# A fused linear-attention and SwiGLU kernel: the gates of the last tiles taken in PSUM in a fixed ScalarE order, and a reordered load stage

## The chip, the cores and the metric

The kernel runs on one core of a Trainium2 chip. The metric is the device time of one execution in microseconds (us). Before the change the median of three runs is 1623.3 us (1622.49, 1623.55, 1623.3). The engines are TensorE (PE; its weight loads are PEld), VectorE (DVE), ScalarE (ACT), GpSimd (POOL) and SyncE (SP, which issues most DMAs).

## The reference

```python
def _A_ref(x, wqkv, w_phi, wo):                    # S=2048, D=576, 32 heads of 18
    q, k, v = ...(x @ wqkv)
    pq, pk = einsum(q, w_phi), einsum(k, w_phi)
    phi_q = concat([softmax(pq), softmax(-pq)]);  phi_k = the same of pk
    o = (phi_q @ (phi_k^T v)) / (phi_q @ sum(phi_k) + 1e-6)
    return o @ wo

def _B_ref(x, w_gate, w_up, w_down):               # F=4608
    return (silu(x @ w_gate) * (x @ w_up)) @ w_down

xn = layernorm(x)
out = x + _A_ref(xn, ...) * silu(_B_ref(xn, ...))
```

All inputs are fp32. x is 2048 x 576, w_gate and w_up 576 x 4608, w_down 4608 x 576.

## The kernel before, in words

**Precision.** Every fp32 operand of a matmul is kept as two rounded parts, a high part (a cast, mostly on ScalarE) and a low part (the operand less the high part, on VectorE or GpSimd). A product is then three matmuls: high x high, high x low, low x high. D = 576 is four chunks of 128 and a remainder of 64; two 32-row halves of the remainder are stacked with their low parts in one chunk, so that the remainder takes one 96-row matmul (`split_rows` L63 and the 32-row subtractions L66, L223, L278 make that chunk).

**Load stage** (L158 to L285, the first 67 us). Rows of x come in four blocks of 512 (four tiles `xn` of 128 rows each), in the order 2, 3, 0, 1. `norm_stats` (L179 to L193) takes the statistics of a tile on VectorE, then for a whole set of tiles one square root on ScalarE (L188) and five small VectorE steps. `norm_block` (L195) scales the tiles alternately on VectorE (L201) and ScalarE (L198), GpSimd repeats the last 64 columns (L204), PE transposes (L213) into PSUM tiles `tp`, three buffers, and ScalarE and VectorE split the result into `X` tiles (L215, L216). For the third transposed tile ScalarE casts two pieces (L220), copies the tile to `xr` in SBUF (L221), and GpSimd subtracts the 32 rows (L223); `xr` also goes to DRAM (L224). Between the blocks, `early_weights` (L102) splits the weights of the first two column tiles f = 0, 1 of w_gate and w_up, and `early_tile` (L119) already computes h for block pair i = 1: gate matmuls into `pe`, silu on ScalarE (L126), up matmuls into `pe`, product on VectorE (L130), store by GpSimd (L131). There, two PSUM banks `pe` alternate, so a matmul can wait for the silu or the product that empties its bank. `fold` (L235 to L243) multiplies w_k (into KVWH/KVWL) and w_q (into QH/QL) with the feature matrix PHI on PE (L242). The loop at L266 to L278 loads the six pieces of w_v into tiles `wst` (five buffers, shared with the w_q loads at L232): cast to KVWH on ScalarE (L274), KVWL on GpSimd for four (L276), the 32-row remainder on VectorE for two (L278). Behind it stand the w_q loads, the statistics of blocks 0 and 1 together, block 0, the fold of w_q, block 1. The scheduler moves what is marked high priority ahead.

**Behind it**: the k/v tiles (their first matmuls, `p`, take PSUM that the `tp` tiles held), the q tiles, and then gate/up and down products in two halves of the rows with Strassen's scheme (L741, L866). This is 67 to 1598 us.

**The end** (second half, i = 1, L862 to L913). Eight tiles of 128 rows, t = 4, 5, 6, 7, 0, 1, 2, 3, get their last two down products. `tile_of` (L882) fills a PSUM tile with the sum so far, `acc` (a ScalarE copy, L893), and adds 12 matmuls of 288 columns (`three`, L866). `finish` (L834) takes silu from PSUM to `acc` (ScalarE, L837), multiplies by the attention part (VectorE, L838), adds x (L839, VectorE for even t, GpSimd for odd ones) and stores (SP, L840). PSUM tile `pd` has two buffers. The last tile, t = 3 ("fine"), is in two halves, in `py` and `pw`, each with its own finish. Fills have high priority; the rest is in the order in which the scheduler finds it ready.

## Time and profile before

| what | value |
|---|---|
| three runs | 1622.49, 1623.55, 1623.3 us; median 1623.3 |
| the profiled execution's own time | 1622.04 us |
| its span in the trace | 1620.2 us |
| mean granted TensorE clock | 0.998 |
| PE busy | 1605.8 us, 99% of the span, 9411 instructions |
| DVE, ACT, POOL busy | 1175.9, 726.3, 660.8 us |
| DMA moved | 268.28 MB, mean 166 GB/s |

Times in the trace are microseconds from the span's start. The device time of an execution is some 1.8 us longer than its span. An engine's busy time leaves out the issue of DMAs, semaphores and branches. In a row of a timeline, the number in brackets is how long the engine had been idle and which instruction ended that; "x3" is three like instructions run together, and their time is that of the group. The lines themselves stand in the prediction.

### The profile page before, as it was taken

How to read it: one execution, taken by the hardware profiler on the slowest of the kernel's cores; microseconds unless marked ns; L12 is line 12 of the kernel's file. 1: busy time of each engine (PE TensorE's matmuls, PEld its weight loads, DVE VectorE, ACT ScalarE, POOL GpSimd, SP SyncE). 2: the span in 40 equal slices, each digit the busy share in tenths (PEclk: the TensorE clock that was granted, in tenths of full speed). 3: DMA queues.
4: the chain of work that ended last, by engine and by line, in shares of the span. 5: the costliest groups of instructions: out<-in, count | busy, mean ns of one | idle time of the engine just before them, and what ended most of it. 6: DMA issues, size and time to landing. Idle time of an engine off the chain costs nothing.

```text
span 1620.2 us, 25277 instructions
## 1 busy us (share of the span) xinstructions
PE 1605.8 (99%) x9411; PEld 1428.2 (88%) x9412; DVE 1175.9 (73%) x1727; ACT 726.3 (45%) x1399; POOL 660.8 (41%) x710
## 2 busy tenths in 40 slices
PE   9999999999999999999999999999999999999998
PEld 6899998999988888888888888888888888888887
DVE  7777769898856778877777778634667656666578
ACT  5633345544445654444444444454343333333334
POOL 3676652334115635644535435223324314133132
PEclk9999999999999999999999999999999999999999
DMA  9522243436347454555545453965445654555435
GB/s 325 172 80 82 98 144 105 125 105 191 121 158 255 165 180 163 175 171 181 177 169 191 168 188 114 335 210 148 151 137 154 187 174 157 177 181 175 142 116 176
DMA packets 121420, 268.28 MB, mean 166 GB/s; under 512 B 12754, under 2 KB 53842, under 8 KB 119506
## 3 DMA queue, kind: packets, MB, share of 16 engines
q1 hardware_dynamic: 105852, 244.73, 45.9%
q0 software_dynamic: 3552, 12.59, 2.7%
q10 hardware_dynamic: 11894, 9.35, 1.8%
q8 instruction: 74, 1.21, 0.3%
q14 instruction: 48, 0.39, 0.1%
HBM read 167.53 MB, written 99.09 MB: 165 GB/s over the span
## 4 chain that ended last, share of the span: by engine, by line
PE 94%; DVE 3%; DMA 1%; ACT 1%; issue 0%; POOL 0%; SPq 0%; POOLq 0%; ACTq 0%
PE pd L866 25%; PE px L741 25%; PE pw L741 12%; PE p L94 7%; PE py L741 6%; PE pe L94 5%; PE p L641 4%; PE kvp L320 2%; PE po L621 2%; PE vx L408 1%; PE pt L615 1%; PE vw L408 1%; PE vy L94 1%; PE vx L94 1%; DVE stats L183 1%
## 5 line engine op out<-in xcount | busy, mean ns | idle before, releaser
L866 PEld LDWEIGHTS pd<-dw,hh 128*128 128x128 f32 x3036 | 431.0, 188 | 22.3 <-DVE X L997 0.9
L866 PE MATMUL pd<-dw,hh 128*128 128x288 f32 x3036 | 446.7, 297 | 0.7 <-DVE X L997 0.4
L741 PE MATMUL px<-X,w 128*128 128x512 f32 x1512 | 390.4, 393 | 0.0
L741 PEld LDWEIGHTS px<-X,w 128*128 128x128 f32 x1512 | 275.0, 188 | 52.7 <-ACT s L770 2.2
L741 PE MATMUL pw<-X,w 128*128 128x512 f32 x744 | 191.8, 393 | 0.0
L741 PEld LDWEIGHTS pw<-X,w 128*128 128x128 f32 x744 | 139.2, 189 | 30.9
L775 DVE TENSOR_TENSOR s<-pw,s 128x512 f32<-128x512 f32 x126 | 86.5, 688 | 101.0 <-ACT s L770 89.5
L997 DVE TENSOR_TENSOR acc<-pd,acc 128x576 f32<-128x576 f32 x128 | 96.2, 752 | 84.4 <-PE pd L866 84.2
L770 ACT COPY s<-px 128x512 f32<-128x512 f32 x126 | 73.9, 586 | 160.6 <-PE px L741 160.6
L61 DVE TENSOR_TENSOR hh<-ha,hh 128x512 fp32r<-128x512 f32 x140 | 111.9, 825 | 22.8 <-ACT hh L60 21.3
L60 ACT CAST hh<-ha 128x512 fp32r<-128x512 f32 x140 | 82.7, 619 | 87.0 <-PE pd L866 72.0
L969 POOL TENSOR_TENSOR hb<-hb 128x512 f32<-128x512 f32 x34 | 46.5, 1367 | 164.9 <-DVE hb L787 159.2
L94 PE MATMUL pe<-X,wh 128*128 128x512 f32 (+1 forms) x340 | 108.5, 399 | 1.9 <-POOL X L223 0.8
L61 DVE TENSOR_TENSOR w<-ld,w 128x512 fp32r<-128x512 f32 (+1 forms) x96 | 80.2, 835 | 36.6 <-ACT w L60 35.3
L741 PE MATMUL px<-X,wt 96*128 96x512 f32 x252 | 99.5, 395 | 0.0
L741 PE MATMUL py<-X,w 128*128 128x512 f32 x378 | 98.0, 394 | 0.0
L956 POOL TENSOR_TENSOR h<-ha,hb 128x512 f32<-128x512 f32 x34 | 44.4, 1305 | 125.1 <-DVE ha L791 95.2
L982 POOL TENSOR_TENSOR ha<-ha 128x512 f32<-128x512 f32 x34 | 52.6, 1563 | 98.7 <-DVE hh L61 98.7
L60 ACT CAST w<-ld 128x512 fp32r<-128x512 f32 (+1 forms) x96 | 52.7, 549 | 88.1 <-POOL ld L729 56.4
L795 ACT COPY py<-px 128x512 f32<-128x512 f32 x63 | 36.0, 572 | 106.4 <-PE px L741 83.4
L726 POOL TENSOR_TENSOR ts<-ld 128x256 f32<-128x256 f32 x32 | 27.4, 856 | 129.4 <-issue 73.3
L741 PEld LDWEIGHTS py<-X,w 128*128 128x128 f32 x378 | 67.8, 188 | 11.3
(275 smaller groups left out, 3249.2 us busy)
## 6 DMA issues: line engine op xcount, KB each, us to landing
w_dram<-w SPq DMA_DIRECT2D x90, 512.0 KB
w<-w_dram SPq DMA_DIRECT2D x90, 512.0 KB
wt<-t_dram SPq DMA_DIRECT2D x62, 336.0 KB
ld<-in_B_w_gu SPq DMA_DIRECT2D x32, 512.0 KB
X<-sum_dram SPq DMA_DIRECT2D x8, 1280.0 KB
rt<-in_B_w_down SPq DMA_DIRECT2D x33, 288.0 KB
rb<-in_B_w_down SPq DMA_DIRECT2D x33, 288.0 KB
w_dram<-w SPq DMA_DIRECT2D x30, 256.0 KB
```

Source lines behind the costliest of these rows:

```text
L60: nc.scalar.copy(hi, src)
L61: nc.vector.tensor_sub(lo, src, hi)
L94: last = nc.tensor.matmul(ps, l, r, start=n == 0, stop=n == len(pairs) - 1)
L641: nc.tensor.matmul(ps[:, 0:HALF], a[0:w, g, jc], bw[0:w, g, n], start=k == 0, stop=k == 3 * NG - 1)
L741: nc.tensor.matmul(ps, l, r, start=first and n == 0, stop=last and n == len(mm) - 1, skip_group_check=True)
L770: snaps.append(nc.scalar.copy(t, ps))
L775: nc.vector.tensor_add(t, ps, t)
L866: nc.tensor.matmul(ps, l, r, start=first and n == 0 and m == 0, stop=n == len(hs) - 1 and m == 2, skip_group_check=True)
L956: sub(s, g["h"][0][0], g["h"][0][1])
L969: nc.gpsimd.tensor_add(a21, a21, g["h"][1][1])
L982: sub(a12, a12, g["h"][0][0])
L997: nc.vector.tensor_add(a2, pd[:, :, 0:HALF], a2)
```

## The change

Two places in the program differ; all rows between them stand in the same order on every engine.

**Load stage.** (1) For block 3 the two 32-row subtractions go from GpSimd (out of `xr`) to VectorE (out of PSUM, new L227), with high priority. (2) The w_v pieces are loaded and cast in the order (0,0), (0,1), (1,0), (1,1), (0,2), (1,2); the KVWL subtractions on GpSimd are issued behind the last remainder of the early weights. (3) The statistics and norms of block 0 are written ahead of the two remainders of KVWH, which are issued behind the sixth VectorE scaling. (4) A one-column silu is issued right behind the square root.

**End.** `finish` becomes `end`: silu in place in PSUM, product from PSUM into `acc`, adds on GpSimd, the last tile's on VectorE behind both products. A tile's end is issued behind the fill of the next but one, and a fill behind the silu of the one before. Tiles t = 6 and t = 1 use two buffers `px` in halves in place of a `pd`.

On VectorE in the load stage, where block 3's third transposed tile meets the early weights of f = 1 (`X12_66`, `X13_67` are block 3's chunks, `wl_384` and `wh_383` the split of the first weight tile, `stats`/`mv` the norms of blocks 0 and 1), before:

```order
L216 TENSOR_TENSOR X13_67<-tp_354,X13_67 128x1024
L184 BN_AGGR mv_106<-stats_105 128x2
L183 BN_STATS stats_105<-xn_414 128x6
L65 TENSOR_TENSOR wl_384<-raw_382,wh_383 128x512
L66 TENSOR_TENSOR wh_383<-raw_382,wh_383 32x2x128
L183 BN_STATS stats_105<-xn_414 128x6
```

and now:

```order
L218 TENSOR_TENSOR X13_67<-tp_354,X13_67 128x1024
L227 TENSOR_TENSOR X12_66<-tp_365,X12_66 32x512
L227 TENSOR_TENSOR X13_67<-tp_365,X13_67 32x512
L65 TENSOR_TENSOR wl_384<-raw_382,wh_383 128x512
L66 TENSOR_TENSOR wh_383<-raw_382,wh_383 32x2x128
L186 BN_AGGR mv_106<-stats_105 128x2
```

The two remainders stand directly ahead of the weight split, and one statistics step and a mean that stood ahead of it come behind.

On VectorE a little further, from the second weight tile (`wl_391`, `wh_390`) to the root, before (`h_679` is the product of an early tile, L278 makes a remainder of KVWH):

```order
L65 TENSOR_TENSOR wl_391<-raw_389,wh_390 128x512
L66 TENSOR_TENSOR wh_390<-raw_389,wh_390 32x2x128
L130 TENSOR_TENSOR h_679<-pe_664,h_679 128x512
L278 TENSOR_TENSOR KVWH_97<-wst_400,KVWH_97 32x576
L184 BN_AGGR mv_106<-stats_105 128x2
L183 BN_STATS stats_105<-xn_420 128x6
```

and now:

```order
L65 TENSOR_TENSOR wl_391<-raw_389,wh_390 128x512
L132 TENSOR_TENSOR h_680<-pe_665,h_680 128x512
L66 TENSOR_TENSOR wh_390<-raw_389,wh_390 32x2x128
L186 BN_AGGR mv_106<-stats_105 128x2
L185 BN_STATS stats_105<-xn_418 128x6
L185 BN_STATS stats_105<-xn_420 128x6
```

The product h has moved ahead of the 32-row subtraction, the remainder of KVWH is gone from here, and more of the statistics is left behind this point.

On GpSimd in the load stage, before:

```order
L204 COPY xn<-xn 128x128 x8
L131 DMA h_dram<-h 128x512
L223 TENSOR_TENSOR X_66<-xr,X_66 32x512
L223 TENSOR_TENSOR X_67<-xr,X_67 32x512
L276 TENSOR_TENSOR KVWL<-wst,KVWH 128x576 x3
L131 DMA h_dram<-h 128x512
L276 TENSOR_TENSOR KVWL<-wst,KVWH 128x576
L204 COPY xn<-xn 128x128 x6
```

and now:

```order
L206 COPY xn<-xn 128x128 x8
L133 DMA h_dram<-h 128x512
L281 TENSOR_TENSOR KVWL<-wst,KVWH 128x576 x4
L133 DMA h_dram<-h 128x512
L206 COPY xn<-xn 128x128 x2
L133 DMA h_dram<-h 128x512
L206 COPY xn<-xn 128x128 x14
```

The remainders of block 3 are gone and the four KVWL stand together. On PE, the first k/v matmul was `p_787`, which waits for a VectorE subtraction of block 1; now `p_788` comes first, and it waits for ScalarE's copy to `xr`, since its PSUM is that of the tile which this copy reads.

On ScalarE at the end (`pd`, `px`, `py`, `pw` are the PSUM tiles; a COPY is a fill, an ACTIVATE a silu), the last rows before:

```order
L837 ACTIVATE acc<-pd 128x2x288
L893 COPY pd<-acc 128x2x288
L837 ACTIVATE acc<-pd 128x2x288 x2
L837 ACTIVATE acc<-py 128x288
L837 ACTIVATE acc<-pw 128x288
```

and now:

```order
L893 ACTIVATE pd<-pd 128x2x288
L914 COPY pd<-acc 128x2x288
L893 ACTIVATE px<-px 128x288 x2
L914 COPY py<-acc 128x288
L914 COPY pw<-acc 128x288
L893 ACTIVATE pd<-pd 128x2x288
L893 ACTIVATE py<-py 128x288
L893 ACTIVATE pw<-pw 128x288
```

The fills of `py` and `pw`, which stood near the start of the end (PE ran a few of t = 3's matmuls early), now come last, and each fill is held behind the silu ahead of it.

```diff
@@ -63,7 +63,7 @@
     def split_rows(hi, lo, src):
         nc.scalar.copy(hi, src)
         nc.vector.tensor_sub(lo, src[:, :, 0:2], hi[:, :, 0:2])
-        nc.vector.tensor_sub(hi[64:96, :, 2], src[64:96, :, 2], hi[64:96, :, 2])
+        return nc.vector.tensor_sub(hi[64:96, :, 2], src[64:96, :, 2], hi[64:96, :, 2])
 
     xpool = ctx.enter_context(tc.tile_pool(name="xpool", bufs=1))
     dram = ctx.enter_context(tc.tile_pool(name="dram", bufs=1, space=bass.MemoryType.DRAM))
@@ -99,6 +99,8 @@
     pes = ctx.enter_context(ExitStack())
     eps = pes.enter_context(tc.tile_pool(name="eps", bufs=2, space=PSUM, side="right"))
 
+    rests = []
+
     def early_weights(f, *behind):
         parts = []
         for m in (0, 2):
@@ -110,7 +112,7 @@
                 for b in behind:
                     order.enter_context(tc.issue_after(b.ins))
                 with tc.high_priority():
-                    split_rows(hi, lo, raw)
+                    rests.append(split_rows(hi, lo, raw))
             parts.append((hi, lo))
         return parts
 
@@ -174,7 +176,7 @@
                         nc.sync.dma_start(xn[:, 0:D], xf[i * P:(i + 1) * P, :])
                     return xns
 
-                roots, norms = [], []
+                roots, norms, scales = [], [], []
 
                 def norm_stats(bs, xns):
                     t = slice(4 * bs[0], 4 * bs[-1] + 4)
@@ -198,8 +200,8 @@
                             norms.append(nc.scalar.activation(xn[:, 0:D], xn[:, 0:D], AF.Identity,
                                                               bias=rt[:, i:i + 1], scale=rs[:, i:i + 1]))
                         else:
-                            nc.vector.tensor_scalar(xn[:, 0:D], xn[:, 0:D], mv[:, i, 0:1], rs[:, i:i + 1],
-                                                    op0=ALU.subtract, op1=ALU.mult)
+                            scales.append(nc.vector.tensor_scalar(xn[:, 0:D], xn[:, 0:D], mv[:, i, 0:1], rs[:, i:i + 1],
+                                                                  op0=ALU.subtract, op1=ALU.mult))
                         for k in range(2):
                             nc.gpsimd.tensor_copy(xn[:, D + k * P:D + (k + 1) * P].rearrange("p (j n) -> p j n", j=4),
                                                   xn[:, 512 + 32 * k:544 + 32 * k].unsqueeze(1).to_broadcast([P, 4, 32]))
@@ -220,7 +222,11 @@
                             nc.scalar.copy(dst[m][:, 2], ps[:, m])
                         copy = nc.scalar.copy(xr, ps)
                         for m in range(2):
-                            nc.gpsimd.tensor_sub(dst[m][32:64, 2], xr[32:64, m], dst[m][32:64, 2])
+                            if b == 3:
+                                with tc.high_priority():
+                                    nc.vector.tensor_sub(dst[m][32:64, 2], ps[32:64, m], dst[m][32:64, 2])
+                            else:
+                                nc.gpsimd.tensor_sub(dst[m][32:64, 2], xr[32:64, m], dst[m][32:64, 2])
                             nc.scalar.dma_start(x_dram[i, :, :, 2 * j + m].rearrange("s p n -> p s n"),
                                                 xr[:, m].rearrange("p (s n) -> p s n", s=4))
                     return last, rest, copy
@@ -262,23 +268,26 @@
                 fold(wk, KVWH[:, :, :, 0:D], KVWL[:, :, :, 0:D])
                 _, _, copy = norm_block(3, xns[4:8])
                 first_weights.append(early_weights(1, copy))
-                wv = []
-                for n in range(6):
-                    wv.append(prep.tile([P, 6 * P], F32, name="wst", bufs=5))
-                    nc.sync.dma_start(wv[n][:, 0:D], w_v[:, n // 3, n % 3])
+                wv, places = [], [(0, 0), (0, 1), (1, 0), (1, 1), (0, 2), (1, 2)]
+                for k, c in places:
+                    wv.append(prep.tile([P, 6 * P], F32, name="wst", bufs=5)[:, 0:D])
+                    nc.sync.dma_start(wv[-1], w_v[:, k, c])
                 xns = load_x(0) + load_x(1)
-                for n in range(6):
-                    k, c = divmod(n, 3)
-                    src, vh = wv[n][:, 0:D], KVWH[:, k, c, D:2 * D]
+                for (k, c), src in zip(places, wv):
                     with tc.issue_after(copy.ins):
-                        nc.scalar.copy(vh, src)
-                    if c < 2:
-                        nc.gpsimd.tensor_sub(KVWL[:, k, c, D:2 * D], src, vh)
-                    else:
+                        nc.scalar.copy(KVWH[:, k, c, D:2 * D], src)
+                for (k, c), src in zip(places[0:4], wv):
+                    with tc.issue_after(rests[-1].ins):
+                        nc.gpsimd.tensor_sub(KVWL[:, k, c, D:2 * D], src, KVWH[:, k, c, D:2 * D])
+                norm_stats([0, 1], xns)
+                with tc.high_priority(), tc.issue_after(roots[-1].ins):
+                    nc.scalar.activation(stats[:, 0, 0, 0:1], mv[:, 0, 0:1], AF.Silu)
+                norm_block(0, xns[0:4])
+                for (k, c), src in zip(places[4:6], wv[4:6]):
+                    vh = KVWH[:, k, c, D:2 * D]
+                    with tc.issue_after(scales[5].ins):
                         nc.vector.tensor_sub(vh[64:96], src[64:96], vh[64:96])
                 wq = load_fold(1)
-                norm_stats([0, 1], xns)
-                norm_block(0, xns[0:4])
                 fold(wq, QH, QL)
                 norm_block(1, xns[4:8])
                 for f in range(2):
@@ -831,14 +840,6 @@
     def halves_of(ap):
         return ap.rearrange("p (a n) -> p a n", a=2)
 
-    def finish(t, k, pd, sx, eng):
-        r0 = HS + t * P
-        a = acc[:, t // 4 * 2:t // 4 * 2 + 2, t % 4][:, k]
-        nc.scalar.activation(a, pd, AF.Silu)
-        nc.vector.tensor_mul(a, a, halves_of(sx[:, 0])[:, k])
-        eng.tensor_add(a, a, halves_of(sx[:, 1])[:, k])
-        nc.sync.dma_start(halves_of(of[r0:r0 + P, :])[:, k], a)
-
     def late_finish(t):
 
         y = fw.tile([P, D], F32, name="ts")
@@ -879,29 +880,52 @@
                 split(w[:, 0], w[:, 1], raw[:, n])
                 ws.append(w)
 
+        silu, fills, ends = [], [], []
+
+        def end(t, pd):
+            fine = t == HT // 2 - 1
+            a = acc[:, t // 4 * 2:t // 4 * 2 + 2, t % 4]
+            s, x = (halves_of(final[t // 2][:, t % 2, m]) for m in range(2))
+            o = halves_of(of[HS + t * P:HS + t * P + P, :])
+            parts = list(enumerate(pd)) if isinstance(pd, list) else [(slice(0, 2), pd)]
+            with tc.high_priority(), tc.issue_after(fills[-1].ins):
+                for k, p in parts:
+                    silu.append(nc.scalar.activation(p, p, AF.Silu))
+                    done = nc.vector.tensor_mul(a[:, k], p, s[:, k])
+            with tc.issue_after(done.ins):
+                for k, p in parts:
+                    (nc.vector if fine else nc.gpsimd).tensor_add(a[:, k], a[:, k], x[:, k])
+                    nc.sync.dma_start(o[:, k], a[:, k])
+
         def tile_of(t, hs):
             fine = i == 1 and t == HT // 2 - 1
-            if fine:
-                pd = [fps.tile([P, BT], F32, name=n, bufs=1)[:, 0:HALF] for n in ("py", "pw")]
+            apart = fine or (i == 1 and t in (HT // 2 + 2, 1))
+            if apart:
+                names = ("py", "pw") if fine else ("px", "px")
+                both = None
+                pd = [fps.tile([P, BT], F32, name=n, bufs=names.count(n))[:, 0:HALF] for n in names]
             else:
                 both = fps.tile([P, 2, 512], F32, name="pd", bufs=2)[:, :, 0:HALF]
                 pd = [both[:, k] for k in range(2)]
             c = slice(t % 4 * P, t % 4 * P + P)
             a2 = acc[:, t // 4 * 2:t // 4 * 2 + 2, t % 4]
-            with tc.high_priority() if i else ExitStack():
-                for k in range(2 if fine else 1):
-                    nc.scalar.copy(pd[k] if fine else both, a2[:, k] if fine else a2)
+            with tc.high_priority() if i else ExitStack(), tc.issue_after(silu[-1].ins) if silu else ExitStack():
+                for k in range(2 if apart else 1):
+                    fill = nc.scalar.copy(pd[k] if apart else both, a2[:, k] if apart else a2)
+            fills.append(fill)
+            if ends:
+                ends.pop()()
             for k in range(2):
                 n = slice(k * HALF, (k + 1) * HALF)
                 three(pd[k], [(h[:, 0, c], h[:, 1, c]) for h in hs], [(w[:, 0, n], w[:, 1, n]) for w in ws],
                       False)
-                if fine:
-                    finish(t, k, pd[k], final[t // 2][:, t % 2], nc.vector)
             if i == 0:
                 nc.scalar.activation(a2, both, AF.Silu)
                 nc.scalar.dma_start(y_dram[t], a2)
-            elif not fine:
-                finish(t, slice(0, 2), both, final[t // 2][:, t % 2], (nc.vector, nc.gpsimd)[t % 2])
+                return
+            ends.append(lambda: end(t, pd if apart else both))
+            if fine:
+                ends.pop()()
 
         for r in (1, 0) if i else (0, 1):
             hs = []
```

## The prediction

> **What bounds the kernel now.** I read the page first (its span and the shares of the chain that ended last), then busy time by stretches, then the timelines of the load stage and of the end.
>
> ```profile
> span 1620.2 us, 25277 instructions
> PE 94%; DVE 3%; DMA 1%; ACT 1%; issue 0%; POOL 0%; SPq 0%; POOLq 0%; ACTq 0%
> ```
>
> TensorE is 94% of the chain. Three of the five stretches into which I cut the span (start:end, length, then the busy time of PE, PEld, DVE, ACT and POOL with counts, clock, DMA share, GB/s):
>
> ```profile
> 31.10:67.30 36.20, 33.57 (x199) 28.07 (x198) 29.41 (x52) 26.04 (x37) 18.31 (x27) 1.00 0.76 261
> 67.30:1597.80 1530.50, 1528.57 (x8948) 1366.17 (x8947) 1105.94 (x1590) 671.60 (x1320) 627.76 (x652) 1.00 0.49 160
> ...
> 1612.80:1620.20 7.40, 0.00 (x0) 0.00 (x0) 4.01 (x6) 0.41 (x2) 1.84 (x1) 0.63 0.45 159
> ```
>
> In the middle, PE is idle for 1.93 of 1530.5 us. The change leaves every engine's order there as it was, apart from the first k/v matmuls, so the middle passes on whatever shift reaches it. What can be won lies in two places: 36.20 - 33.57 = **2.63 us** of PE idle in the load stage that the change touches, and the 7.40 us behind the last matmul. All the working below is in this execution's own time (1622.04 us, span 1620.2); the difference is then taken off the median, 1623.3.
>
> **The load stage: what stands there.** PE's timeline; the bracket is the idle time before the row, and what released it.
>
> ```profile
> 35.50 0.73 PE L94 MATMUL pe<-X,wh 96*128 96x512 f32 x2 [0.83 <-POOL X L223]
> ...
> 44.11 0.47 PE L94 MATMUL pe<-X,wh 128*128 128x512 f32 x1 [0.82 <-DVE h L130]
> ...
> 48.47 0.87 PE L213 MATMUL tp<-ident,xn 128*128 128x128 f32 x3 [0.85 <-DVE xn L201]
> ...
> 54.98 5.52 PE L242 MATMUL tp<-PHI,wst 126*128 126x126 f32 x48
> ...
> 62.62 1.04 PE L213 MATMUL tp<-ident,xn 128*128 128x128 f32 x8
> ...
> 67.33 0.30 PE L94 MATMUL p<-KVWH,X 128*128 128x288 f32 x1
> ```
>
> Three stalls, 0.83 + 0.82 + 0.85 = 2.50 us, are nearly all of the idle time. VectorE and GpSimd over the same time:
>
> ```profile
> 22.42 0.42 DVE L66 TENSOR_TENSOR KVWH<-tp,KVWH 32x252 fp32r<-32x252 f32 x1
> ...
> 33.00 1.21 DVE L216 TENSOR_TENSOR X<-tp,X 128x1024 fp32r<-128x1024 f32 x1
> ...
> 34.57 1.43 DVE L65 TENSOR_TENSOR wl<-raw,wh 128x512 fp32r<-128x512 f32 x1
> 36.03 1.39 DVE L66 TENSOR_TENSOR wh<-raw,wh 32x256 fp32r<-32x256 f32 x1
> ...
> 41.72 1.53 DVE L66 TENSOR_TENSOR wh<-raw,wh 32x256 fp32r<-32x256 f32 x1
> ...
> 44.00 0.75 DVE L278 TENSOR_TENSOR KVWH<-wst,KVWH 32x576 fp32r<-32x576 f32 x1
> ...
> 44.91 0.77 DVE L183 BATCH_NORM_STATS2 stats<-xn 128x6 f32<-128x288 f32 x2
> ...
> 47.75 1.55 DVE L201 TENSOR_SCALAR xn<-xn,mv,rs 128x576 f32<-128x576 f32 x3
> ```
> ```profile
> 34.18 2.96 POOL L223 TENSOR_TENSOR X<-xr,X 32x512 fp32r<-32x512 f32 x2
> 37.31 1.43 POOL L276 TENSOR_TENSOR KVWL<-wst,KVWH 128x576 fp32r<-128x576 f32 x1 [0.17 <-POOL X L223]
> ...
> 48.46 2.47 POOL L204 COPY xn<-xn 128x128 f32<-128x128 f32 x6 [2.16 <-DVE xn L201]
> ```
>
> A 32-row subtraction of 252 elements takes 0.42 us, one of 576 takes 0.75: 1.02 ns an element, so 0.68 us for 512.
>
> **The load stage, step by step.** *Block 3's remainders.* GpSimd loses 2.96 us, VectorE gets 2 x 0.68. It starts behind the L216 that ends at 34.21: 34.9 and 35.6. PE, free at 35.50 - 0.83 = 34.67, has in the new order two more matmuls of the same tile to run first (0.73 us for two at 35.50, their latency included). I count the 0.83 us stall as gone (bounds 0.3 to 0.83).
>
> *The weight splits.* `wl` and `wh` at 34.57 and 36.03 took 1.43 and 1.39 us while GpSimd was busy. With GpSimd empty I give them the nearest uncovered prices, 0.68 and 0.42: they end at 36.7 rather than 37.42, behind two more instructions. The second tile's `wl` then waits out a KVWL to 40.0, and the product h (L130) runs at about 40.7 to 41.3, while PE comes to its bank at 44.11 - 0.82 - 0.83 = 42.5. The second stall, 0.82 us, goes, and nothing else is late there.
>
> *The KVWL subtractions* are written behind the last remainder, which is VectorE's. In the built order they carry no wait for it, only those for their load and cast. So they still run beside VectorE: about 37.2 to 40.0 for two, and two more to 43.8. Queued behind them are h's store and the xn copies (L204), and both are needed later than 43.8.
>
> *The norms.* Before, VectorE came out of wh at 43.25, then did h and one KVWH remainder, to 44.75, and the last statistics, to the root at 46.59, 1.8 us. Now h is done by 41.3, the remainder is put off, and wh ends at about 42.4. The order leaves two more statistics (0.77) and their mean behind it, so 2.65 us are still to do. The root starts at about **45.06** instead of 46.59, a gain of 1.53.
>
> ```profile
> 46.59 0.21 ACT L188 ACTIVATE rs<-mv 128x8 f32<-128x8 f32 x1 [3.94 <-DVE mv L187]
> 46.81 1.28 ACT L126 ACT_TABLE_LOAD   x1
> ...
> 52.23 1.93 ACT L215 CAST X<-tp 128x1024 fp32r<-128x1024 f32 x2
> ...
> 66.66 1.05 ACT L221 COPY xr<-tp 128x1024 f32<-128x1024 f32 x1
> ```
>
> *The silu table.* Its 1.28 us load follows the root in both programs, beside VectorE's chain. What leaves ScalarE behind it is one silu (0.3 us net of the dummy). So the cast of the first transposed pair comes at root + 5.35 rather than + 5.64, and the fold of w_q, which waits for the tile that this frees, starts 1.53 + 0.25 = 1.78 earlier, at 53.2.
>
> *What is given back.* The two KVWH remainders now stand between the scaling of xn and h on VectorE, and may exclude GpSimd's copies for 2 x 0.75, as wl and wh at 34.57 were held up beside GpSimd. I put the further PE waits there at 0.2 (bounds 0 to 0.8) and count them inside the time from 46.8 to 53.2. Block 1's transposes then come at 61.06 rather than 62.62. The first k matmul now waits for the xr copy: in this trace that copy ends at 66.66 + 1.05 = 67.71, which is 5.09 us behind the transposes' start, while p started 4.71 behind it. So the wait moves p to 61.06 + 5.12 = 66.2 instead of 67.33. PE would have been there 0.8 us sooner: this is the new stall, behind which all of k and v is queued. **Load stage: -1.1 us.** Bounds: 0, if copies and the xr copy take all, and -2.6, if all the idle time goes.
>
> **The end.** From the chain that ended last, then groups (line, engine, operation, count: shortest/median/longest in ns), then single rows of VectorE, GpSimd and SP:
>
> ```profile
> 1601.47 0.52 PE py L866 x2
> ...
> 1605.37 6.48 PE pd L866 x48
> ```
> ```profile
> L893 ACT COPY pd<-acc x7: 637/644/644, 1598.5 to 1609.3; 128x576 f32<-128x576 f32 x7
> L837 ACT ACTIVATE acc<-pd x7: 643/652/655, 1601.7 to 1611.9; 128x576 f32<-128x576 f32 x7
> ```
> ```profile
> L997 DVE TENSOR_TENSOR acc<-pd,acc x128: 740/756/759, 593.4 to 1600.1; 128x576 f32<-128x576 f32 x128
> ```
> ```profile
> 1603.21 0.75 DVE L838 TENSOR_TENSOR acc<-acc,X 128x576 f32<-128x576 f32 x1
> ...
> 1605.96 1.58 DVE L838 TENSOR_TENSOR acc<-acc,X 128x576 f32<-128x576 f32 x1 [0.54 <-ACT acc L837]
> ```
> ```profile
> 1605.50 1.43 POOL L839 TENSOR_TENSOR acc<-acc,X 128x576 f32<-128x576 f32 x1 [8.26 <-DVE acc L838]
> ...
> 1612.73 1.91 POOL L839 TENSOR_TENSOR acc<-acc,X 128x576 f32<-128x576 f32 x1 [2.21 <-issue]
> ```
> ```profile
> 1604.78 12.55 SPq L840 DMA_DIRECT2D out<-acc  x9
> ```
>
> *PE.* A tile is 12 matmuls at 6.48 / 48 = 0.135, so 1.62 us. ScalarE's fixed loop is silu 0.65 + fill 0.64 + 0.15 of latency = 1.44, and fits with 0.18 to spare. PE loses its early work on t=3, but behind the first tile it starts at 1601.5, on the split of h that releases it at 1601.47 now, with 7 x 12 = 84 matmuls to go: 1601.5 + 11.34 = 1612.84, as now (1612.8). I cost this at nothing; past the 0.18 of slack each tile would add the excess.
>
> *VectorE* multiplies from PSUM. The nearest row is L997, 756 ns over 128 instructions and never above 759, while the SBUF form took 1.58 beside a GpSimd add. So 0.75, and 7 adds leave VectorE.
>
> *GpSimd* gets the 7 adds. The first starts as the first product ends, 1603.21 + 0.75. Five whole ones at 1.43 and two in halves (4 x 0.80, from the row below) are 10.35, plus 0.3 between them: t=2's sum ends at 1614.65. This, not PE, now sets the end.
>
> ```profile
> L374 POOL TENSOR_TENSOR h<-sraw x1: 804/804/804, 83.7 to 83.7; 128x288 f32<-128x288 f32 x1
> ```
> ```profile
> L840 SPq DMA_DIRECT2D out<-acc x9: 402/534/621, 1604.8 to 1616.9; - x9
> ```
>
> *SP* issues t=2's store and the last two behind it: 0.53 + 0.40 + 0.40, to 1616.0. VectorE's last two adds (288 columns, 0.45 each by the 0.75 of a 576) are under this: pw's silu and product, some 0.45 each, are done by 1613.8, and the adds run at the latest from 1614.65 to 1615.6. Before, the last issue ended at 1604.78 + 12.55 = 1617.33; what follows, 2.87 us to the span's end, stays. **End: -1.3 us.** Bounds: -2.3 if GpSimd is never behind (products at 1613.77, one add, two issues), and +2.1 by what follows.
>
> What the adds cost depends on whether the product from PSUM holds them up. Beside products of the SBUF form an add took 1.91 at 1612.73, not 1.43; at that price seven adds take 3.4 us more, and the end is 2.1 slower instead of 1.3 faster. Against it stand the 128 rows of L997, which never met such a delay. The Trainium skill, "SBUF — State Buffer", section "SBUF: two separate sides", says that VectorE and GpSimd share one port pair as an exclusive lock, held for a whole instruction by a VectorE operation with two SBUF inputs. By that rule the product from PSUM, with one SBUF input, leaves the adds alone, and the sum keeps its 1.3; the trace agrees where it shows both, in VectorE's 1.58 at 1605.96, which ends 0.6 us behind GpSimd's 1.43 of 1605.50.
>
> **Sum.** 1.1 + 1.3 = 2.4 us: span 1617.8, profiled time 1619.6, and 1623.3 - 2.4 = **1620.9**.
>
> **The rivals.**
> - *More is won.* The xr copy is early enough because ScalarE is freer, and GpSimd hardly delays the end. For it: ScalarE has 10 us idle in the load stretch. Against it: both waits are in the built order. All 2.6 of the idle and 1.3: 1623.3 - 3.9 = 1619.4.
> - *The load stage gives nothing.* Copies blocked by the remainders and p behind xr take back what the root gains; the end's 1.3 is left: 1622.0. For it: GpSimd's copies have no slack at the third stall (xn at 47.75, its copy at 48.46, PE behind it). Against it: the root really is earlier. To this belongs the case that the change doesn't do what it says, since nothing holds the KVWL subtractions off VectorE's norms.
> - *Slower: the fourth load of w_q comes late.* Its buffer is now freed by a remainder that ends near 48.8, rather than by the last KVWL, which ends just ahead of the root, and its issue stands behind a 1280 KB store (issues, KB each, us to landing):
>
> ```profile
> a_dram<-X SPq DMA_DIRECT2D x2, 1280.0 KB
> ...
> h_dram<-h POOLq DMA_DIRECT2D x3, 256.0 KB, 4.8
> ```
>
> The fold needs it at 53.2 + 4.1 (three quarters of 5.52) = 57.3, so 8.5 us after its issue at 48.8. The nearest landing is 4.8 us for 256 KB; with 1280 KB ahead at the stretch's 261 GB/s it is up to 9.7. The gain is gone if it lands 10.9 us after its issue; at 12 us PE is 3.5 late, and the time is 1623.3 - 2.4 + 3.5 = 1624.4.
> - *Slower: the adds stretch.* GpSimd at 1.91 an add, as above, from 1.62 on already no gain at the end: 1623.3 - 1.1 + 2.1 = 1624.3. For it: the row at 1612.73. Against it: L997.
>
> **How the numbers follow.** Forecast, 1620.9: 0.42. More won, 1619.4: 0.28. Load stage nothing, 1622.0: 0.20. Late w_q, 1624.4: 0.04. Stretched adds, 1624.3: 0.04. Something else: 0.02. A measurement of this kernel can tell about 0.2%, 3.2 us, from no change. Below 1620.1 lie most of the second case and the edge of the first: faster 0.32. Above 1626.5 lies only a part of the two slower cases and of the rest: 0.04. Same: 0.64. The bounds of the terms (load 0 to -2.6, end +2.1 to -2.3) together, without the far corners that need both, give 1618.5 to 1622.8.
>
> **What would show it.** Right: no stall before the 96-row matmuls nor at h; a root near 45.1; p near 66.2 with a wait for xr ahead of it; PE's end near 1612.8 less the shift; seven GpSimd adds back to back, and the last store's issue some 3.2 us behind PE's end instead of 4.5. Wrong: the root at 46 or later, a fold that waits for its load, a GpSimd add above 1.5, or PE waiting for fills at the end.

## The result and the profile after

| | runs | median, us | lowest to highest | ratio to before, 95% interval |
|---|---|---|---|---|
| before | 18 | 1623.1 | 1622.44 to 1626.62 | |
| changed | 18 | 1620.28 | 1619.05 to 1622.54 | 0.9981 [0.9974, 0.9987] |

The change makes the kernel 2.8 us faster by the medians, 0.19% by the ratio, with an interval of 1.3 to 2.6 thousandths. The forecast was 2.4 us. The execution that was profiled is the longest of the 18, 1622.54 us with a span of 1620.7, so its span cannot be set against that of before. Its stretches can. The cuts are at the same instructions in both programs: from the first early-tile matmul behind block 3's transposes to the first k matmul, from there to the first down product behind the last gate/up product (six matmuls, then tile t = 4), to PE's last matmul, to the end. Start:end and length, then busy times in the order of the prediction's stretches:

```profile
32.65:67.55 34.90, 33.42 (x200) 28.06 (x198) 28.13 (x55) 26.46 (x38) 15.90 (x25) 1.00 0.79 281
67.55:1600.11 1532.56, 1529.12 (x8949) 1366.50 (x8949) 1106.96 (x1590) 670.79 (x1320) 628.78 (x652) 1.00 0.49 160
1600.11:1615.03 14.92, 14.26 (x103) 13.56 (x101) 10.56 (x17) 11.37 (x24) 8.69 (x8) 1.00 0.48 171
1615.03:1620.70 5.67, 0.00 (x1) 0.00 (x0) 1.92 (x4) 0.40 (x1) 1.40 (x1) 0.88 0.50 179
```

Before, three of these cuts lay at

```profile
31.14 0.48 PE L94 MATMUL pe<-X,wh 128*128 128x512 f32 x1
...
1598.07 0.97 PE L866 MATMUL pd<-dw,hh 128*128 128x288 f32 x6
...
1611.81 0.95 PE L866 MATMUL pw<-dw,hh 128*128 128x288 f32 x6
```

and the fourth at the 67.33 of the prediction's rows. So the four stretches were 67.33 - 31.14 = 36.19, 1598.07 - 67.33 = 1530.74, 14.69 (to 1612.76) and 7.44 us. The load stage got 1.29 us shorter, the middle 1.82 longer, PE's part of the end 0.23 longer, and what follows PE 1.77 shorter. Ahead of the first cut this execution is 1.51 us later than before's. That offset stands in full by the first load of w_v (issued at 18.50 us, before at 16.94), which lies ahead of everything that the change touched. The gain is in the first and the last stretch. The longer middle has to be shown to be none of the change's doing; the second profile of the same kernel, below, has only a part of it.

PE's waits in the load stage. The two stalls of 0.83 and 0.82 us are gone, the one at xn is 0.63 instead of 0.85, and two waits are new, 0.31 at GpSimd's copies of xn and 0.53 at the first k matmul:

```profile
48.37 0.66 PE L215 MATMUL tp<-ident,xn 128*128 128x128 f32 x3 [0.63 <-DVE xn L203]
...
52.25 0.77 PE L215 MATMUL tp<-ident,xn 128*128 128x128 f32 x5 [0.31 <-POOL xn L206]
...
67.55 0.40 PE L94 MATMUL p<-KVWH,X 128*128 128x288 f32 x1 [0.53 <-ACT xr L223]
```

VectorE's rows there. The remainders take 0.64 us each, and `wl` and `wh`, which took 1.43 and 1.39, now take 0.69 and 0.42, started ahead of GpSimd's subtractions:

```profile
32.77 1.23 DVE L218 TENSOR_TENSOR X<-tp,X 128x1024 fp32r<-128x1024 f32 x1
...
35.75 1.28 DVE L227 TENSOR_TENSOR X<-tp,X 32x512 fp32r<-32x512 f32 x2
37.07 0.69 DVE L65 TENSOR_TENSOR wl<-raw,wh 128x512 fp32r<-128x512 f32 x1
37.79 0.42 DVE L66 TENSOR_TENSOR wh<-raw,wh 32x256 fp32r<-32x256 f32 x1
...
40.20 1.25 DVE L65 TENSOR_TENSOR wl<-raw,wh 128x512 fp32r<-128x512 f32 x1
41.48 0.69 DVE L132 TENSOR_TENSOR h<-pe,h 128x512 f32<-128x512 f32 x1
42.20 0.81 DVE L66 TENSOR_TENSOR wh<-raw,wh 32x256 fp32r<-32x256 f32 x1
```

GpSimd's four KVWL subtractions run beside VectorE's second `wl` and `wh`, which are the ones that are still long:

```profile
37.84 6.46 POOL L281 TENSOR_TENSOR KVWL<-wst,KVWH 128x576 fp32r<-128x576 f32 x4 [2.22 <-ACT KVWH L278]
```

ScalarE around the root. The silu that now stands ahead of the square root waited 2.87 us for the store of h to land, which still held its buffer, and the root could start only when its table load behind that silu had ended, at 46.48, though its input was ready at 45.61 (VectorE's L189 ran from 45.44 for 0.17):

```profile
44.57 0.60 ACT L128 ACTIVATE h<-pe 128x512 f32<-128x512 f32 x1 [2.87 <-DMA h_dram<-h]
45.18 1.28 ACT L190 ACT_TABLE_LOAD   x1
46.48 0.21 ACT L190 ACTIVATE rs<-mv 128x8 f32<-128x8 f32 x1
46.70 1.28 ACT L284 ACT_TABLE_LOAD   x1
```

The end: PE's last tile, the groups of the products (L894) and adds (L897), and SP's store issues:

```profile
1603.60 1.87 PE L867 MATMUL pd<-dw,hh 128*128 128x288 f32 x12 [0.48 <-ACT pd L914]
...
1614.07 0.96 PE L867 MATMUL pw<-dw,hh 128*128 128x288 f32 x6
```
```profile
L894 DVE TENSOR_TENSOR acc<-pd,X x5: 751/758/759, 1605.3 to 1614.2; 128x576 f32<-128x576 f32 x5
...
L894 DVE TENSOR_TENSOR acc<-px,X x4: 457/458/458, 1607.1 to 1612.3; 128x288 f32<-128x288 f32 x4
```
```profile
L897 POOL TENSOR_TENSOR acc<-acc,X x9: 800/1398/1432, 1606.1 to 1615.0; 128x576 f32<-128x576 f32 x5, 128x288 f32<-128x288 f32 x4
...
L897 DVE TENSOR_TENSOR acc<-acc,X x2: 447/665/883, 1615.9 to 1616.7; 128x288 f32<-128x288 f32 x2
```
```profile
1607.54 10.61 SPq L898 DMA_DIRECT2D out<-acc  x11
```

No product is longer than 0.76 and no add on GpSimd longer than 1.43. The last store's issue ends at 1618.15, 3.12 us behind PE's last matmul at 1615.03; before it was 4.57. One of VectorE's two last adds took 0.88 instead of 0.45, beside GpSimd's last.

### The profile page after: what moved, and what is told of

It is laid out like the page before. It is cut to its first block, busy times and chain, and to the rows that moved or that the text cites. A ratio compares the mean times of both kernels' runs of the same rounds, so it can differ in the third digit from the quotient of the medians.

```text
span 1620.7 us, 25290 instructions
## 1 busy us (share of the span) xinstructions
PE 1606.0 (99%) x9412; PEld 1429.8 (88%) x9412; DVE 1170.7 (72%) x1727; ACT 726.0 (45%) x1404; POOL 664.7 (41%) x714
## 4 chain that ended last, share of the span: by engine, by line
PE 93%; DMA 3%; DVE 1%; ACT 1%; POOL 1%; issue 1%; SPq 0%; DVEq 0%; ACTq 0%; POOLq 0%
PE pd L867 25%; PE px L750 25%; PE pw L750 12%; PE p L94 7%; PE py L750 6%; PE pe L94 5%; PE p L650 4%; PE kvp L329 2%; PE po L630 2%; PE vx L417 1%; PE pt L624 1%; DMA s_dram<-so 1%; PE vw L417 1%; DMA h_dram<-h 1%; PE tp L248 1%
```

## The experiments

The kernel before ran beside each group on the same chip: 1623.16 us for the first four runs, 1623.14 for the next four, 1623.16 for the last two. Two distances serve below, since offsets ahead of the changed code drop out of them: **X to p**, from the first L216 (L218) of block 3 to the first k matmul, 67.33 - 31.26 = 36.07 before and 67.55 - 32.77 = 34.78 in the changed kernel's first profile; and **PE to end**, from PE's last matmul to the end of the span, 7.44 and 5.67. Where the first of them starts, before:

```profile
31.26 1.22 DVE L216 TENSOR_TENSOR X<-tp,X 128x1024 fp32r<-128x1024 f32 x1
```

### One part at a time: `load_only` and `end_only`

```diff
 load_only: before.py with the change's hunks up to L290
 end_only:  before.py with the hunks of finish/end and tile_of
```

> The load stage of the changed kernel with the end of the kernel before. Theory (the changed kernel's gain is two separate sums, load stage about 1.3 us and end about 1.5 us): 1.3 us faster than before, 0.9992; in the trace, measured from the first early-tile matmul behind the transposes of block 3 (31.14 before, 32.65 after), the first k matmul comes 34.9 us later as in the changed kernel, not 36.2 as before, and the end is as before: last store's issue about 4.5 us behind PE's end. Rival (the profiled gain in the load stage is given back in the middle, where the changed kernel's trace shows 1.5 us of stalls that before's does not): the time is that of before, 1.000, with stalls near 423 and 516 us again.

> The end of the changed kernel with the load stage of the kernel before. Theory of two separate sums: 1.5 us faster than before, 0.9991; no stall of over 0.3 us near 423 and 516 us that before's trace lacks is asked for by it; the span ends 5.7 us behind PE's last matmul, not 7.4. Rival (the end's gain comes only with the earlier load stage, or the whole 2.8 us is from the end): 1.000 or 0.9983.

`load_only`: 1621.82 us, ratio 0.9990 [0.9981, 0.9999], 1.34 us faster. X to p is 67.36 - 32.43 = 34.93, and PE to end 7.59. `end_only`: 1621.06 us, 0.9988 [0.9979, 0.9997], 2.10 faster. X to p is 67.55 - 31.46 = 36.09, as before, and PE to end 5.66. The rows, PE and VectorE of `load_only`, then PE of `end_only`:

```profile
67.36 0.40 PE L94 MATMUL p<-KVWH,X 128*128 128x288 f32 x1 [0.53 <-ACT xr L223]
```
```profile
32.43 1.22 DVE L218 TENSOR_TENSOR X<-tp,X 128x1024 fp32r<-128x1024 f32 x1
```
```profile
423.68 0.41 PE L641 MATMUL p<-WOH,oh 126*128 126x288 f32 x1 [1.06 <-ACT so L649]
...
516.67 1.19 PE L858 MATMUL pd<-dw,hh 128*128 128x288 f32 x7 [0.28 <-DVE hh L61]
```

Both parts gain and each stays in its own stretch. The medians add to 3.44, and the whole change gave 3.28 on the same chip. The intervals reach about 1.5 us to either side, so the medians show that each part gains, and how much is better read from the distances. The stalls near 423 and 516 us come in `end_only`, which has the load stage of before, and not in `load_only`: they come without the new load stage too.

### The changed kernel again: `after_again`

> The changed kernel once more, for a second profile. Theory (the 1.5 us by which block 3's transposes came later in its first profile, and the stalls of 1.09 us at 423.5 and 0.41 us at 516.6, are differences between executions in when DMAs land): the offset and the two stalls come out otherwise, and the span is near 1618.4. Rival (they belong to the changed kernel): the same stalls at the same places, within 0.3 us. In both, the silu ahead of the square root waits for h's store, the root is 1.0 us behind the last statistics, and p waits 0.5 us for the copy to xr.

1619.88 us, 0.9984 [0.9976, 0.9993]; the profiled execution took 1619.28, its span is 1617.4. Of the offset 0.28 us is left (first L218 at 31.54, before 31.26), the stall near 423 is gone, and that near 516 is 0.24. VectorE, ScalarE and PE of this profile:

```profile
31.54 1.23 DVE L218 TENSOR_TENSOR X<-tp,X 128x1024 fp32r<-128x1024 f32 x1
```
```profile
42.74 0.60 ACT L128 ACTIVATE h<-pe 128x512 f32<-128x512 f32 x1 [2.28 <-DMA h_dram<-h]
43.35 1.28 ACT L190 ACT_TABLE_LOAD   x1
44.65 0.21 ACT L190 ACTIVATE rs<-mv 128x8 f32<-128x8 f32 x1
```
```profile
65.72 0.40 PE L94 MATMUL p<-KVWH,X 128*128 128x288 f32 x1 [0.53 <-ACT xr L223]
```

X to p is 34.18 here, 0.60 less than in the first profile. The expectation that the root would be 1.0 us behind its input failed: h's store landed earlier, and the input, ready at 44.55, waited 0.1. Over the nine profiles with this silu ahead of the root (those of the experiments below among them), X to p lies between 34.11 and 34.93, with a mean of 34.46. So the load stage gains 1.1 to 2.0, **1.6 us** in the mean. The spread comes with executions, and the landing of h's store is one part of it. Which of the four edits of the load stage gains how much was not run apart, save for the silu's place below; it rests on the rows.

### Products from SBUF: `sbuf_products`

```diff
-silu.append(nc.scalar.activation(p, p, AF.Silu))
-done = nc.vector.tensor_mul(a[:, k], p, s[:, k])
+silu.append(nc.scalar.activation(a[:, k], p, AF.Silu))
+done = nc.vector.tensor_mul(a[:, k], a[:, k], s[:, k])
```

> The changed kernel, but silu goes from PSUM to SBUF and the product reads two SBUF inputs, as before the change; all adds but the last tile's stay on GpSimd. Theory (two SBUF inputs on VectorE and GpSimd exclude each other, so the PSUM form of the product is what keeps seven adds on GpSimd cheap): adds of 1.6 to 1.9 us and products of 1.4 to 1.8, the last add 2 to 3.5 us later than in the changed kernel, the whole 2 to 3 us slower than it, about 1622.5 to 1623.5. Rival (where the product is read from costs nothing; the move of the adds and the order are what counts): within 0.5 us of the changed kernel, 1620.3.

1622.9 us, 0.9998 [0.9989, 1.0006]: 3.0 us slower than `after_again` on the same chip, nearly the whole gain. Its products and adds:

```profile
L894 DVE TENSOR_TENSOR acc<-acc,X x11: 444/1361/1911, 1601.6 to 1614.4; 128x288 f32<-128x288 f32 x6, 128x576 f32<-128x576 f32 x5
```
```profile
L897 POOL TENSOR_TENSOR acc<-acc,X x9: 1009/1443/1957, 1602.4 to 1614.1; 128x576 f32<-128x576 f32 x5, 128x288 f32<-128x288 f32 x4
```

The last stretch is what grew: PE to end is 1620.0 - 1611.41 = 8.59, where `after_again` has 5.64. PE's part is unchanged, 1611.41 - 1596.46 = 14.95 against 14.91. ScalarE's order, the fills and the split of the adds are the changed kernel's; only where silu writes and the product reads differs. VectorE's products pay most: a half one takes 1.36 us in the mean where the changed kernel has 0.46, and GpSimd's five whole adds take 1.65 where they had 1.40. So without products from PSUM the end does not gain: with seven adds on GpSimd and products from SBUF it was 1.2 us worse behind PE than in the kernel before. Whether products from PSUM gain as much with the adds split as before, and what the fixed ScalarE order and `px` add, no run shows. The rows agree with the rule that the prediction cites from the Trainium skill ("SBUF — State Buffer", section "SBUF: two separate sides"), by which a VectorE operation with two SBUF inputs and a GpSimd operation that reads SBUF exclude each other.

### The copy to xr first: `xr_first`

```diff
+copy = nc.scalar.copy(xr, ps) if b == 1 else None
 for m in range(2): nc.scalar.copy(dst[m][:, 2], ps[:, m])
-copy = nc.scalar.copy(xr, ps)
+copy = copy or nc.scalar.copy(xr, ps)
```

> The changed kernel, but for block 1 ScalarE makes the copy to xr ahead of the two casts of 512 columns instead of behind them. Theory (the first k matmul waits for that copy, 0.53 us in both profiles, and all of k and v is queued behind it): the wait is gone, p comes 0.5 us earlier from the transposes of block 1 (4.95 us before, 4.4 now), and the whole is 0.5 us faster than the changed kernel, about 1619.6. Rival (PE would then wait as long for something else, or the shift is lost in the middle): p's distance from the transposes unchanged within 0.1, or the time within 0.2 of the changed kernel.

1620.23 us, 0.9984 [0.9975, 0.9993]. PE:

```profile
66.75 0.40 PE L94 MATMUL p<-KVWH,X 128*128 128x288 f32 x1 [0.53 <-ACT X L222]
```

The wait is the same 0.53, with another name behind it, and p stands 4.95 us behind block 1's transposes (61.80) as before the swap. In both orders p waits for ScalarE's last read of the PSUM tile. The theory named the wrong cause: the copy mattered only because it came last. The time did not move either, where 1619.6 had been expected.

### The silu behind the root: `silu_late`

```diff
-early_tile(f, 1, first_weights[f], store=nc.gpsimd, hold=None if f else norms[3])
+early_tile(f, 1, first_weights[f], store=nc.gpsimd, hold=roots[-1] if f else norms[3])
```

> The changed kernel, but the early tiles' silus of f = 1 are issued behind the square root, as the kernel before had it. Theory (the silu ahead of the root waits for h's store to land and so holds the root up by 0.1 to 1.0 us, with hardly any gain for PE): the root comes 13.1 us or less behind X's first subtraction of block 3 in each execution, but the bank that this silu would have emptied holds PE back, so the whole is within 0.5 us of the changed kernel. Rival (the silu's early place is what makes the load stage faster, since it frees the bank and leaves ScalarE for the norms): xn's fold comes 0.5 to 1.0 us later, and the whole is 0.5 to 1.0 us slower than the changed kernel.

1619.97 us, 0.9984 [0.9975, 0.9992], 0.1 from `after_again`. ScalarE and PE:

```profile
45.04 0.21 ACT L190 ACTIVATE rs<-mv 128x8 f32<-128x8 f32 x1 [2.84 <-DVE mv L189]
```
```profile
46.92 0.87 PE L215 MATMUL tp<-ident,xn 128*128 128x128 f32 x3 [1.11 <-DVE xn L203]
```

The root now waits for its input alone, and comes 13.52 us behind X's first subtraction; with the silu ahead of it, it came between 13.05 and 13.86. The bound of 13.1 was wrong. PE waits longer at xn, 1.11, and X to p is 66.22 - 31.52 = 34.70, within the others' range. That h's store can hold the root up is real in single executions (0.9 us in the first), but in this one profile taking it away wins nothing that shows.

### The last sums from PSUM, the last stores from ScalarE

```diff
 psum_sum:
-done = nc.vector.tensor_mul(a[:, k], p, s[:, k])
+done = nc.vector.tensor_mul(p if fine else a[:, k], p, s[:, k])
-(nc.vector if fine else nc.gpsimd).tensor_add(a[:, k], a[:, k], x[:, k])
+(nc.vector if fine else nc.gpsimd).tensor_add(a[:, k], p if fine else a[:, k], x[:, k])
 act_store:
-nc.sync.dma_start(o[:, k], a[:, k])
+(nc.scalar if fine else nc.sync).dma_start(o[:, k], a[:, k])
 xr_psum = xr_first with psum_sum; psum_act_store = psum_sum with act_store
```

> The changed kernel, but for the last tile the product stays in PSUM and the add reads it there, so that neither VectorE instruction has two SBUF inputs. Theory (VectorE's last two adds are held by GpSimd's add of t = 2): the two adds take 0.45 us each right behind the products, and no longer end behind GpSimd's add; the last store's issue then follows the store of t = 2 on SP, and the span ends 0.3 to 0.5 us earlier behind PE's last matmul (5.65 now). Rival (the adds wait for something else, such as the stores of other tiles, or SP is the limit): the adds start at the same distance, and the span's end is unchanged within 0.1.

> Both of these: xr's copy first for block 1, and the last tile's sums out of PSUM. Theory of separate sums: 0.8 to 1.0 us faster than the changed kernel, about 1619.2, 0.9976 of the kernel before. Rival (one of the two is worth nothing): 1619.6 to 1619.9.

> The changed kernel, but ScalarE, which has no work left, issues the last tile's two stores in place of SP. Theory (behind PE the end is a chain of t = 2's product, GpSimd's add of 1.40 and three store issues on SP, one behind the other): the last issue ends 0.5 us earlier behind PE's last matmul, 2.6 us instead of 3.13, since VectorE's adds, which end behind GpSimd's, now set it; the span's end follows by 0.3 to 0.5. Rival (not the issues but the landing of the last stores sets the end): the span still ends 5.6 us behind PE's last matmul.

> The same with the last tile's sums read from PSUM, so that neither GpSimd nor SP stands before them. Theory: the adds end 1.65 us behind PE's last matmul as in the run with the sums from PSUM alone, ScalarE's second issue ends at 2.4 to 2.6, SP's issue of t = 2's store at 2.0, and the span's end is 0.6 to 1.0 us earlier than in the changed kernel, 4.7 to 5.0 behind PE: about 1619.4. Rival (the landing sets the end): 5.6 us behind PE, 1620.2.

`psum_sum`: 1619.92 us, 0.9981 [0.9972, 0.9990]. `xr_psum`: 1620.26, 0.9982 [0.9973, 0.9990]. VectorE, then SP, of `psum_sum`:

```profile
1613.52 0.45 DVE L897 TENSOR_TENSOR acc<-py,X 128x288 f32<-128x288 f32 x1
1613.89 0.45 DVE L897 TENSOR_TENSOR acc<-pw,X 128x288 f32<-128x288 f32 x1
```
```profile
1605.19 10.62 SPq L898 DMA_DIRECT2D out<-acc  x11
```

Both adds take 0.45 though GpSimd's last add runs from 1612.69 to 1614.09, beside the whole of the first and the start of the second. So the hold hung on the second SBUF input, and it is gone. But the last issue ends at 1615.81, 3.13 us behind PE (1612.68), exactly as without it: SP issues t = 2's store when GpSimd is done and the other two behind it. The theory's first half holds, its gain does not; VectorE was not what the end waited for. `xr_psum` put together two parts that are each worth nothing; 1619.2 had been expected, or 1619.6 to 1619.9 with one of them worth nothing.

`act_store`: 1619.84 us, 0.9979 [0.9970, 0.9988]. `psum_act_store`: 1619.52, 0.9979 [0.9970, 0.9987]. ScalarE's queue in the one and in the other:

```profile
1614.71 0.97 ACTq L898 DMA_DIRECT2D out<-acc  x2
```
```profile
1613.22 0.83 ACTq L898 DMA_DIRECT2D out<-acc  x2
```

The last issues end 2.73 and 2.16 us behind PE (1612.95 and 1611.89) instead of 3.13, but the spans end 5.65 and 5.21 behind it instead of 5.64. From the last issue to the end it takes 2.92 and 3.05 us now, 2.5 in the changed kernel. Of 0.4 us of earlier issue nothing is seen, as the rival said, and of 1.0 us less than half; the 4.7 to 5.0 expected of `psum_act_store` was missed. Why, the DMA engines show. Their share and GB/s are the last two figures of a row; `after_again`, `act_store` and `psum_act_store`:

```profile
1614.34:1616.06 1.72, 0.00 (x0) 0.00 (x0) 0.00 (x0) 0.00 (x0) 0.00 (x0) 1.00 0.97 343
```
```profile
1615.54:1617.25 1.71, 0.00 (x0) 0.00 (x0) 0.00 (x0) 0.00 (x0) 0.00 (x0) 0.65 0.97 345
```
```profile
1614.02:1615.74 1.72, 0.00 (x0) 0.00 (x0) 0.00 (x0) 0.00 (x0) 0.00 (x0) 1.00 0.96 340
```

The last three stores, t = 2's and two halves, are 0.59 MB, and the DMA engines move them in one stretch of 1.7 us, with nothing just before it and nothing behind it; 1.35 us after its end the span ends. In the first two runs alike it starts 2.6 us behind PE, and t = 2's store, whose issue ends 1.98 behind PE in both, is first in it. Issuing the two halves earlier behind that one only lets them stand in line. In `psum_act_store` ScalarE issues the first half ahead of it, the stretch starts 2.1 behind PE, and the end comes 0.43 earlier. So in these runs the end is set by when the last stretch of stores starts. The best version tried is `psum_act_store`, 0.4 us shorter than the changed kernel behind PE; its interval against before overlaps that of the changed kernel.

## Why the prediction was right, step by step

*The load stage* was forecast at 1.1 and is 1.6 in the mean of the profiles (1.29 in the first), 1.34 by the medians of `load_only`.

- *Remainders, wl and wh*: forecast 1.36, 0.68 and 0.42 us, measured 1.28, 0.69 and 0.42. Both stalls went, as said.
- *KVWL not held off VectorE*: as said; four took 6.46 us beside `wl` and `wh`.
- *The root*: forecast 45.06, which is 13.80 us behind X's first subtraction. Measured 13.05 to 13.86 over those nine profiles, 13.4 in the mean, so the gain of this term was put 0.4 too small. The first profile's 13.71 agrees with the forecast by luck, since two errors cancel there. VectorE left the second `wh` at 43.01, 10.24 behind X where 11.14 was forecast, and with the 2.60 that followed (forecast 2.65) the root's input was ready 0.96 earlier than forecast; then the root waited 0.87 for the table load, because the silu ahead of it waited for h's buffer, a wait that the forecast missed altogether.
- *From the root to the first transposed pair's cast*: forecast 5.35, measured 51.72 - 46.48 = 5.24.
- *The wait at p*: forecast 5.12 us behind the transposes with 0.8 of waiting, measured 4.95 with 0.53. Its cause was put too narrowly; `xr_first` has shown it to be the last of ScalarE's reads of that PSUM tile.
- *The late load of w_q*, the slower rival, did not come about. The fourth load was issued later than before (at 50.16 in the first profile, where before its issue was through at 46.64), but the fold waited for no load in any of these profiles.

*The end* was forecast at 1.3 and is 1.54 in the first profile, 2.1 by the medians of `end_only`.

- *PE at nothing* was wrong by 0.2. Without its early matmuls of t = 3 it waits at the second tile for the fill (0.48 at 1603.60), which stands behind a cast in ScalarE's order; from the last cut to PE's last matmul it takes 14.92 instead of 14.69. The prediction named a wait for fills at the end as a sign that it was wrong, and this sign came, at a price of 0.23 us net.
- *Products and adds*: forecast 0.75 and 1.43, measured 0.758 and 1.40, never held up. `sbuf_products` has shown that the end's gain does not come without this step.
- *What sets the end*: forecast 3.2 us from PE to the last issue, measured 3.12. The forecast blamed GpSimd's backlog; in fact GpSimd had been idle for 0.18 before its last add and waited for t = 2's product, so the chain is t = 2's product, add and store issue, and then the DMA traffic of the last three stores. The two chains came out within 0.2 of each other, which is luck.
- *Behind the last issue* the forecast kept 2.87; it is 2.55. This part is no constant: in the changed kernel the stores' traffic starts behind the first of the last three issues, not behind the last. From the last byte moved to the end of the span it takes 1.7 us before and 1.4 in the changed kernel's first profile; why that is shorter is not shown. This unforecast gain of 0.32 and PE's unforecast loss of 0.23 nearly cancel, so the end's total is nearer to the forecast than its terms are.

Of the other signs of being wrong, none held: the root stands at 46.48 in the first profile, but that execution was 1.51 us late from the start; the fold waited for no load, and no add on GpSimd took over 1.43.

Of the rivals, "more is won" lies 0.9 below the measured time and the forecast 0.6 above it. The time alone cannot tell the forecast from that rival, and the traces put the result between them: 1.6 + 1.5 = 3.1 us, where the forecast has 2.4 and the rival 3.9. The middle of the program, on which all of this had to pass through unchanged, varied by itself: 1530.74, 1532.56 and 1531.13 us in the profile before and the two after, more than either term's error.

## What to carry to other kernels

Where VectorE and GpSimd share a chain of elementwise work, let VectorE's instructions read one operand from PSUM: with the adds on GpSimd, that was worth 3.0 us over eight tiles here, and without it handing the adds to GpSimd did not pay. When PE waits for a PSUM tile, ask which reader of the tile is done last: reordering the reads changed the name in the profile and not the wait. Before mending a held engine, ask what is late next: the adds at the end were held for 0.4 us and freeing them won nothing, because the store of another tile, behind GpSimd's add, set when the last stores could start to move.

## What the runs showed of the hardware

Executions differed here by up to 1.6 us in when the first tiles of x were through: the first subtraction of block 3 stood between 31.23 and 32.80 us in the seven profiles with one and the same load stage, and at 32.77 and 31.54 in the two profiles of the changed kernel. Five of the ten profiles with the new load stage or a variant of it were late (32.3 to 32.8) and neither of the two with the old one; two are too few to say whether the old one is ever late. A stall of about 1.1 us near 423 us came in two of all twelve, once with the old load stage and once with the new. For a change of 2 to 3 us the distances between two instructions of one trace were a better measure than a span.

The activation that follows a table load of 1.28 us started 0.02 us behind its end (45.18 + 1.28, then 46.48), so this switch of tables cost the load and no more.
